# Sinkhorn weights loaded one expert ahead, block sums and input preparation a step sooner, and another order of the tail

## The chip, the cores and the metric

The kernel runs on one core of a Trainium2 chip. A core has a matrix engine (TensorE, PE in the profile; PEld are its weight loads), a vector engine (VectorE, DVE), an activation engine (ScalarE, ACT), a general engine (GpSimd, POOL) and a small engine whose queue here issues most of the DMA transfers (SyncE, SP). Each engine works through its own instructions in order and waits on semaphores where it needs another's result. The metric is the device time of one execution in microseconds; the lower the better.

## The reference

2304 tokens of 512 channels pass through three stages. The attention has random features and is no part of what follows.

```python
def _moe_ref(x, w_gate, w1, w2):           # MoE1: 8 experts, all of them for every token
    P = np.exp(logits - max)               # logits = x @ w_gate
    for _ in range(8):                     # Sinkhorn: rows and columns in turn
        P /= P.sum(1, keepdims=True) + 1e-09
        P /= P.sum(0, keepdims=True) + 1e-09
        P *= N / E
    for e in range(E):
        out += P[:, e:e+1] * (np.maximum(x @ w1[e], 0.0) @ w2[e])
def _moe2_ref(x, w_skip, w_gate, w1, w2):  # MoE2: one expert per token
    do = x @ w_skip > 0                    # the other tokens pass unchanged
    e_idx = argmax(x[do] @ w_gate)         # gate = softmax value of the chosen expert
    out[do] = x + gate * (np.maximum(x @ w1[e_idx], 0.0) @ w2[e_idx])
```

w1[e] is 512x1024 and w2[e] 1024x512, in float32.

## The kernel before

**Tiling.** Float32 operands are split into a high and a low part, and each product is made of three matmuls (high by high, high by low, low by high). The 2304 tokens are 18 tiles of 128, in 6 groups of 3 (384 columns) and 3 passes of 6 tiles. MoE1 is a loop over 96 steps n = (pass p, expert e, i), 4 steps per expert, 32 per pass. Pass 0 (to step 31) also builds block combinations of the weights and keeps them in DRAM (`w1c`, `w2c`). Passes 1 and 2 (steps 32 to 63 and 64 to 95) run `fast` with these: seven block products in place of eight, both for x@w1 (`product`, L291) and for h@w2 (`prod2`, L996). In a fast step TensorE runs the seven `product` of step n and, as `sec`, the seven `prod2` of step n-1. The mark of a step in the trace is ScalarE's copy at L1085, after the first product.

**Weighing.** Since the second product is linear, the Sinkhorn weight P[token, e] is put on the hidden block: `weigh` applies relu on ScalarE (L1048) and multiplies on GpSimd by `pw` (L1049). `pw` is one expert's weights for the pass's 768 tokens, spread over all 128 partitions. `load_pw` (L967) reads it from DRAM by one DMA of 384 KB, in rows of 512 bytes. Then come combinations on GpSimd (`comb`, L1053), the split into high and low part (`hi_a` on ScalarE, L1058; `lo_a` on VectorE, L1061), and the block products. Their sums are added into the block buffers `ebuf` by VectorE (L1017).

**SyncE's queue.** All weights come through SyncE's queue in program order: `fetch_w1(n+1)` at a step's start (four DMAs, L160), `fetch_w2(n+1)` behind the step's code (L174, L176). Each DMA waits there until its buffer is free, and holds those behind it. In the kernel before `load_pw` has one buffer and stands behind `fetch_w2` in the last step of an expert (i == 3), for the step that follows.

**Between passes.** `prep_x` (L248) makes the seven input blocks of the next pass during the last expert's steps; its first piece is three subtractions on GpSimd (L258 to L260). `fin` (L1022) combines the block sums of a pass into its output: five pieces, each run by a `next(fz, None)` in the step after the first of the new pass (step 65 for pass 1), and after the loop for pass 2. `route(g)` chooses the experts of MoE2 for a group; its pieces run whenever `pump()` is called, three times per fast step.

**Tail.** After the last step come its `prod2`, `fin(2)`, the last routing pieces, and MoE2 in slots of up to 128 tokens of one expert. Slots 0 and 1 have a known expert and run beside the last routing. `load_slot` loads w1 and w2 as halves `r1[0]`, `r1[1]`, `r2[0]`, `r2[1]`, for slot 0 from GpSimd's queue; `split` makes the parts (cast on ScalarE L1283, low part L1284); `xsplit` transposes and splits a slot's tokens (L1304 to L1306); `products` (L1294) are 12 or 6 matmuls. The count of tokens per expert (L1396) is turned on VectorE (L1399 to L1436) into registers, from which slots 2 and on take their expert.

Of the kernel before, what the change touches and what calls it, by code (L numbers as in the profile page):

```python
# [21 lines left out]
def attn_moe_moe_kernel(  # L22
# [645 lines left out]
    ps_y = yst.enter_context(tc.tile_pool(name="ps_y", bufs=1, space=PSUM))  # L668
# [231 lines left out]
    def second(n, t):  # L900
        if not 0 <= n < ns_:
            return
        p, e, i = steps[n]
        if i == 0:
            ys[t] = ps_y.tile([P, DM], F32, tag=f"y{t}", name=f"y{t}")
# [12 lines left out]
        if i < KI - 1:  # L918
            return
        T = p * 2 * GT + t  # L920
        sc = Pm[:, T, e : e + 1]
        if e == 0:
            acc[t] = ebuf[0][:, t, :]
            if p == 0:
                nc.scalar.copy(acc[t], ys[t])
            else:
                nc.vector.tensor_scalar(acc[t], ys[t], sc, None, OP.mult)
        else:
            if p == 0 and e == 1:
# [56 lines left out]
    def prod2(n, j):  # L986
        if not yb:
            yb.extend(ps_y.tile([P, DM], F32, tag=f"y{t}", name=f"y{t}") for t in range(2 * GT))
# [30 lines left out]
    def fin(p):  # L1019
        eb = ebuf[p % 2]  # L1020
        e1, e6, e7, e5 = eb[:, :GT, :D2], eb[:, :GT, D2:], eb[:, GT:, :D2], eb[:, GT:, D2:]
        add = lambda o, x: nc.vector.tensor_tensor(o, x, o, OP.add)  # L1022
# [8 lines left out]
        yield  # L1031
        add(e7, e6)
        yield
        add(e6, e5)
        add(e5, e7)
# [31 lines left out]
    def fast(n, x_next, fz, pump):  # L1067
# [31 lines left out]
        pump()  # L1099
# [53 lines left out]
    for n, (p, e, i) in enumerate(steps):  # L1153
# [7 lines left out]
        if e == E - 1 and p + 1 < NP:  # L1161
# [37 lines left out]
        if p:  # L1199
            fz = fin(p - 1) if p > 1 and e == 0 and i == 1 else iter(())  # L1200
            fast(n, x_next, fz, pump)
            fetch_w2(n + 1)
            if i == KI - 1:
                load_pw(*steps[n + 1][:2]) if n + 1 < ns_ else None
            continue

        def after(k):
# [7 lines left out]
            if k == 5 and 1 < n < N0 - 1:  # L1215
                split_sum_w2(n)
# [15 lines left out]
    for a in (1, 6, 5):  # L1232
        split_a2(ns_ - 1, a)
# [3 lines left out]
    wst.close()  # L1237


    z_p = ctx.enter_context(tc.tile_pool(name="z", bufs=1))  # L1240
    w_p = ctx.enter_context(tc.tile_pool(name="wz", bufs=9))
    NS = FF // 2
    KH = KF // 2

# [3 lines left out]
    xn += pair([P, DM], F32, "xn3", 3 - NE)  # L1248
    xhs = pair([P, KD, P], F32R, "xhs")
    xls = pair([P, KD, P], F32R, "xls")  # L1250
# [4 lines left out]
    r2 = pair([P, KH, DM], F32, "r2")  # L1255
    r1 = pair([P, KD, NS], F32, "r1")

    def load_slot(e, cond, eng=nc.sync):
        for i in range(4):
# [39 lines left out]
    def xsplit(s):  # L1299
        if s == NSLOT:  # L1300
            return
        px = m_bank()
        for c in range(KD):
            nc.tensor.transpose(px[:, c * P : (c + 1) * P], xn[s % 3][:, c * P : (c + 1) * P], ident)  # L1304
        nc.scalar.copy(xhs[s % 2], px)
        nc.vector.tensor_tensor(  # L1306
            xls[s % 2], px.rearrange("p (c t) -> p c t", c=KD), xhs[s % 2].bitcast(F32), OP.subtract
        )

    wa, wb = {}, {}  # L1310

    def split_a(s, r, c):
        if not 0 < s < NE:
            wa[c, r] = split(r1[r][:, c, :], "w1", nc.gpsimd if (r, c) in ((0, 3), (1, 0), (1, 3)) else nc.vector)
# [6 lines left out]
    def slot(s):  # L1321
        x = (xhs[s % 2], xls[s % 2])
        py = pys[s % 2]
# [17 lines left out]
        p1 = ps_1.tile([P, 512], F32, tag="p1", name="p1")  # L1341
# [10 lines left out]
        p1 = ps_1.tile([P, 512], F32, tag="p1", name="p1")  # L1352
# [6 lines left out]
        yield  # L1359
        products(py, hts[0], lambda c: wb[c], h0, True, False)  # L1360
# [10 lines left out]
    load_slot(reg_at(reg0, 0, [ET.Pool], E - 1), None, nc.gpsimd)  # L1371
# [4 lines left out]
    for s in range(NE):  # L1376
        xsplit(s)
    for _ in fin(NP - 1):
# [18 lines left out]
    next(early[0])  # L1397
# [40 lines left out]
    for _ in early[0]:  # L1438
        pass
# [49 lines left out]
```

## Time and profile before

| what | value |
|---|---|
| median of 3 runs | 1956.0 us (1951.95 to 1956.86) |
| the profiled execution | 1957.7 us |
| its span, first to last instruction | 1956.1 us |
| TensorE busy | 1826.4 us (93%) |
| VectorE busy | 1390.6 us (71%) |
| GpSimd busy | 899.4 us (46%) |
| ScalarE busy | 864.0 us (44%) |
| granted TensorE clock, mean | 0.966 |

Times in the views are microseconds from the span's start. A row of the timeline gives start, duration, engine, line, operation, written tile <- read tiles, shape, count of merged instructions, and in brackets the idle time before it with what released it. A row of the waits gives engine, tile and line that waited, what it waited for, total, times and longest. Granted clock 1.00 is TensorE at full speed.

### The profile page before, as it was taken

What the parts mean: (1) busy time and instruction counts of PE and PEld (TensorE: products, weight loads), DVE (VectorE), ACT (ScalarE), POOL (GpSimd) and SP (SyncE); (2) the same over time, 40 slices, a digit from 0 to 9 for tenths busy, and PEclk for the clock granted to TensorE, in tenths of its full rate; (3) what the DMA queues carried; (4) which work ended last, traced back from release to release, by engine and by line L of the source; (5) the groups of instructions that cost most, each with busy time, mean ns of one, the idle gap of its engine ahead of it and who ended that gap; (6) DMA issues with size and microseconds to landing.
All of it is one profiled execution on the core that took longest, in us unless ns stands there. A gap on an engine that the chain in (4) does not pass through costs nothing. (4 is left out here: it accounts for less than half of the span.)

```text
span 1956.1 us, 31251 instructions
## 1 busy us (share of the span) xinstructions
PE 1826.4 (93%) x11395; PEld 1706.4 (87%) x11395; DVE 1390.6 (71%) x2437; ACT 864.0 (44%) x1856; POOL 899.4 (46%) x876
## 2 busy tenths in 40 slices
PE   8999988999999989999999999888999999999598
PEld 8888777888888878999999999878999999999576
DVE  7768466776677776677667777866777777777577
ACT  5758443444444453343334333432343433334356
POOL 5232134444455453444444444634454444445257
PEclk9989999999999999999999999989999999999799
DMA  7230657888888989667666767556576676665441
GB/s 194 72 91 28 215 207 270 294 294 291 306 307 305 330 314 334 196 244 255 218 223 229 251 224 261 205 185 245 190 246 232 234 259 235 230 238 192 151 165 67
DMA packets 221940, 441.41 MB, mean 226 GB/s; under 512 B 25272, under 2 KB 119576, under 8 KB 221776
## 3 DMA queue, kind: packets, MB, share of 16 engines
q1 hardware_dynamic: 218656, 431.70, 63.9%
q0 software_dynamic: 3120, 7.61, 1.1%
q8 instruction: 92, 1.51, 0.3%
q14 instruction: 72, 0.59, 0.1%
HBM read 320.71 MB, written 132.07 MB: 231 GB/s over the span
## 5 line engine op out<-in xcount | busy, mean ns | idle before, releaser
L291 PE MATMUL m<-xh,w1h 128*128 128x384 f32 x1330 | 456.9, 343 | 16.4 <-DVE c L345 3.0
L291 PE MATMUL m<-xl,w1h 128*128 128x384 f32 x1330 | 453.3, 341 | 0.0
L291 PE MATMUL m<-xh,w1l 128*128 128x384 f32 x1330 | 452.8, 340 | 0.0
L1049 POOL TENSOR_TENSOR c<-c,pw 128x384 f32<-128x384 f32 x192 | 195.2, 1017 | 519.4 <-ACT c L1048 427.0
L291 PEld LDWEIGHTS m<-xh,w1h 128*128 128x128 f32 x1330 | 256.1, 193 | 31.6 <-DVE rc L697 6.2
L996 PE MATMUL y<-w2h,hh 128*128 128x256 f32 x768 | 226.1, 294 | 46.0 <-DVE eb L1017 41.3
L1017 DVE TENSOR_TENSOR eb<-y,eb 128x256 f32<-128x256 f32 x496 | 254.1, 546 | 15.2 <-PE y L996 14.8
L291 PEld LDWEIGHTS m<-xl,w1h 128*128 128x128 f32 x1330 | 256.0, 192 | 8.2
L1061 DVE TENSOR_TENSOR hl<-s,hh 128x384 fp32r<-128x384 f32 x256 | 230.6, 901 | 37.4 <-ACT hh L1058 35.0
L291 PEld LDWEIGHTS m<-xh,w1l 128*128 128x128 f32 x1330 | 254.6, 191 | 0.6 <-DMA w1l<-w1c 0.6
L1061 DVE TENSOR_TENSOR hl<-c,hh 128x384 fp32r<-128x384 f32 x192 | 143.0, 745 | 136.9 <-ACT hh L1058 136.7
L996 PE MATMUL y<-wb,hh 128*128 128x256 f32 x1152 | 220.5, 290 | 4.3 <-DVE eb L1022 2.0
L996 PE MATMUL y<-w2l,hh 128*128 128x256 f32 x768 | 218.8, 285 | 0.0
L996 PE MATMUL y<-w2h,hl 128*128 128x256 f32 x768 | 218.5, 285 | 0.0
L996 PEld LDWEIGHTS y<-w2h,hh 128*128 128x128 f32 x768 | 146.9, 191 | 60.7 <-DVE eb L1017 53.3
L996 PEld LDWEIGHTS y<-wb,hh 128*128 128x128 f32 x1152 | 191.1, 197 | 6.5 <-DVE eb L1022 2.4
L1058 ACT CAST hh<-c 128x384 fp32r<-128x384 f32 x192 | 98.7, 514 | 221.4 <-POOL c L1049 221.4
L1048 ACT ACTIVATE c<-c 128x384 f32<-128x384 f32 x192 | 100.9, 526 | 176.9 <-DVE c L1131 80.3
L1058 ACT CAST hh<-s 128x384 fp32r<-128x384 f32 x256 | 129.9, 509 | 111.2 <-POOL s L1053 111.2
L996 PE MATMUL y<-wb,hl 128*128 128x256 f32 x576 | 165.8, 288 | 0.0
L216 POOL TENSOR_TENSOR wsum<-raw 128x256 f32<-128x256 f32 x32 | 29.4, 919 | 284.7 <-DVE w1l L234 250.1
L1053 POOL TENSOR_TENSOR s<-c,c 128x384 f32<-128x384 f32 x128 | 149.0, 1164 | 14.8 <-DVE c L1123 10.4
(300 smaller groups left out, 3878.5 us busy)
## 6 DMA issues: line engine op xcount, KB each, us to landing
wb<-w2c SPq DMA_DIRECT2D x128, 384.0 KB
w1h<-w1c SPq DMA_DIRECT2D x64, 640.0 KB
w1l<-w1c SPq DMA_DIRECT2D x64, 640.0 KB
w2h<-w2c SPq DMA_DIRECT2D x64, 512.0 KB
w2l<-w2c SPq DMA_DIRECT2D x64, 512.0 KB
w2c<-eb SPq DMA_DIRECT2D x58, 512.0 KB
w1c<-w1h SPq DMA_DIRECT2D x32, 896.0 KB
w1c<-w1l SPq DMA_DIRECT2D x32, 896.0 KB
```

What stands on the lines that cost most here:

```text
L216: nc.gpsimd.tensor_tensor(sm[:, 0], a21, a22, OP.add)
L291: nc.tensor.matmul(ps[:, :GW], x[:, a, c, :], y[:, c, :], start=first and m == 0, stop=m == 3 * KC - 1, skip_group_check=True,)
L996: nc.tensor.matmul(place(k, t), x[:, ts], y,  start=m == 0 and (own or (k, t) == (2, 2) or e == i == 0 and (k, t) in FIRST), stop=m == 2 a ...
L1017: nc.vector.tensor_tensor(dst, src, dst, OP.add)
L1048: nc.scalar.activation(out=t, in_=t, func=AF.Relu)
L1049: nc.gpsimd.tensor_tensor(t, t, pw[steps[n][:2]][:, g], OP.mult)
L1053: nc.gpsimd.tensor_tensor(t, ct[n, x], ct[n, y], op)
L1058: nc.scalar.copy(ha[n, a][0], ct[n, a])
L1061: nc.vector.tensor_tensor(ha[n, a][1], ct[n, a], ha[n, a][0].bitcast(F32), OP.subtract)
```

## The change

There are seven edits.

1. `load_pw` takes its tile from a pool with two buffers, and is called after the first step of expert e for expert e+1, ahead of `fetch_w2`.
2. For one of the two pass changes the first piece of `prep_x` runs in step 62 in place of 63.
3. `fin` of pass 1 makes two of its additions on GpSimd, and two pieces are merged and one is divided.
4. `pump()` is called twice per fast step.
5. In pass 0 the split of summed w2 is done one product earlier (k == 4).
6. In step 88 GpSimd issues the load of slot 0's first half of w1 into the block buffer that is free by then.
7. In the tail slot 0's tokens are split before the last `prod2`; the accumulators of `prod2` are in two pools, so that one is given back early and slot products have banks (`ps_p`) before `fin`; slot 0's first products and slot 1's tokens come before `fin`, all of slot 0 before the count; the memory of `r1[1]`, `xhs` and `xls` is placed first.

```diff
-    ps_y = yst.enter_context(tc.tile_pool(name="ps_y", bufs=1, space=PSUM))
+    tst = ExitStack()
+    ps_y = [yst.enter_context(tc.tile_pool(name="ps_y", bufs=1, space=PSUM))] * (2 * GT)
+    ps_y[2] = ps_y[3] = tst.enter_context(tc.tile_pool(name="ps_t", bufs=1, space=PSUM, side="right"))
...
     def load_pw(p, e):
         if p < NP:
-            t = c_p.tile([P, 2, GW], F32, tag="pw", name="pw", bufs=1)
+            t = w_p.tile([P, 2, GW], F32, tag="wsum", name="pw")
...
-    def fin(p):
+    def fin(p, eng):
...
         add(e6, e1)
         yield
         add_y(e1, 0)
-        yield
         add(e7, e6)
         yield
-        add(e6, e5)
-        add(e5, e7)
+        add(e6, e5, eng)
+        add(e5, e7, eng)
+        yield
         add_y(e7, 2)
         yield
...
         sec(0)
-        pump()
         product(py, 4, 4, n, False)
...
                 nxt[2] = prep_x(nxt[0], nxt[1], xq)
+                if p:
+                    next(nxt[2])
             if i == KI - 1:
                 xp = nxt[2]
-                next(xp)
+                if not p:
+                    next(xp)
...
-            fz = fin(p - 1) if p > 1 and e == 0 and i == 1 else iter(())
+            fz = fin(p - 1, nc.gpsimd) if p > 1 and e == 0 and i == 1 else iter(())
             fast(n, x_next, fz, pump)
+            if i == 0 and n + KI < ns_:
+                load_pw(*steps[n + KI][:2])
             fetch_w2(n + 1)
-            if i == KI - 1:
-                load_pw(*steps[n + 1][:2]) if n + 1 < ns_ else None
+            if n == ns_ - 2 * KI:
+                w1b_0 = w1b[bass.ds(reg_at(reg0, 0, [ET.Pool], E - 1), 1)].rearrange("o (c p) f -> p (o c) f", p=P)
+                nc.gpsimd.dma_start(ebuf[1][:, :KD], w1b_0[:, :, : FF // 2])
             continue
...
-    for a in (1, 6, 5):
-        split_a2(ns_ - 1, a)
+    x0 = xr_p.tile([P, 2, KD, P], F32R, tag="xr", name="x0")
+    xhs, xls = [x0[:, 0]], [x0[:, 1]]
+    r1 = [ebuf[1][:, :KD, :]]
...
+    split_a2(ns_ - 1, 1)
+    xsplit(0)
+    split_a2(ns_ - 1, 6)
+    split_a2(ns_ - 1, 5)
     for j in range(7):
         prod2(ns_ - 1, j)
     mst.close()
     wst.close()
+    tst.close()
...
+            pool = ((0, 3), (1, 0), (1, 3)) if s else ((0, 0), (0, 1), (1, 0), (1, 3))
+            wa[c, r] = split(r1[r][:, c, :], "w1", nc.gpsimd if (r, c) in pool else nc.vector)
...
-    load_slot(reg_at(reg0, 0, [ET.Pool], E - 1), None, nc.gpsimd)
+    load_slot(reg_at(reg0, 0, [ET.Pool], E - 1), None, nc.gpsimd, 1)
...
-    for s in range(NE):
-        xsplit(s)
-    for _ in fin(NP - 1):
+    xsplit(1)
+    early = [slot(s) for s in range(NE)]
+    next(early[0])
+    for _ in fin(NP - 1, nc.vector):
         pass
...
-    early = [slot(s) for s in range(NE)]
     last = [route(NG - 2), route(NG - 1)]
+    for _ in range(2):
+        next(early[0])
...
-    for _ in range(3):
-        next(early[0])
+    for _ in early[0]:
+        pass
...
     nc.tensor.matmul(pm[:1, :E], ones[:, 0:1], cnt[0], start=True, stop=True)
-    next(early[0])
...
-    for _ in early[0]:
-        pass
```

**SyncE at the first step of an expert (step 48).** In the kernel before its queue has these rows; w1h, w1l are the weights of the next step's first product, w2h, w2l and wb those of the second, pw the Sinkhorn weights.

```order
L176 DMA wb_10764<-w2c 128x768
L176 DMA wb_10765<-w2c 128x768
L967 DMA pw<-ptd 128x6x128
L160 DMA w1h<-w1c 128x512
L160 DMA w1l<-w1c 128x512
L160 DMA w1h<-w1c 128x1280
L160 DMA w1l<-w1c 128x1280
L174 DMA w2h<-w2c 128x1024
L174 DMA w2l<-w2c 128x1024
```

After the change the same place reads so.

```order
L176 DMA wb_10769<-w2c 128x768
L176 DMA wb_10770<-w2c 128x768
L160 DMA w1h<-w1c 128x512
L160 DMA w1l<-w1c 128x512
L160 DMA w1h<-w1c 128x1280
L160 DMA w1l<-w1c 128x1280
L969 DMA pw<-ptd 128x6x128
L174 DMA w2h<-w2c 128x1024
```

The load of pw has gone from ahead of the four w1 loads to behind them, and it is now the one for the expert after this.

**GpSimd at the change from step 62 to 63.** The kernel before has the first piece of `prep_x` (L258 to L260) behind the last combinations of step 62.

```order
L1049 TENSOR_TENSOR c_13411<-c_13411,pw 128x384
L1053 TENSOR_TENSOR s<-c_13411,s 128x384
L1053 TENSOR_TENSOR s<-c_13375,c_13472 128x384
L258 TENSOR_TENSOR eb_3036<-xr 128x768
L259 TENSOR_TENSOR eb_3036<-xr,eb_3036 128x768
L260 TENSOR_TENSOR eb_3036<-xr 128x768
L1049 TENSOR_TENSOR c_13562<-c_13562,pw 128x384
```

After the change it stands behind the combinations of step 61, ahead of the first weighing of step 62.

```order
L1051 TENSOR_TENSOR c_13232<-c_13232,pw 128x384
L1055 TENSOR_TENSOR s<-c_13232,s 128x384
L1055 TENSOR_TENSOR s<-c_13196,c_13293 128x384
L258 TENSOR_TENSOR eb_3039<-xr 128x768
L259 TENSOR_TENSOR eb_3039<-xr,eb_3039 128x768
L260 TENSOR_TENSOR eb_3039<-xr 128x768
L1051 TENSOR_TENSOR c_13383<-c_13383,pw 128x384
```

The weighings are L1049 before and L1051 after, the combinations L1053 and L1055; the three subtractions come seven rows sooner among them.

**TensorE in the tail, from the last block product on.** In the kernel before the tokens of both slots are transposed there (L1304), and products of slot 0 (p, L1294) alternate with the transposes of the routing (L721, which read the block buffer that `fin` finishes).

```order
L996 MATMUL y_7889<-wb_19693,hl 128x256
L1304 MATMUL m<-ident,xn 128x128 x8
L1294 MATMUL p_20042<-w1h,xhs_19965 128x512
L1294 MATMUL p_20042<-w1h,xls_19967 128x512
L1294 MATMUL p_20042<-w1l,xhs_19965 128x512
L721 MATMUL m<-ident,eb_3036 128x128 x4
L1294 MATMUL p_20042<-w1h,xhs_19965 128x512
```

After the change, from the last block product, the rows are these.

```order
L998 MATMUL y_7894<-wb_19700,hl 128x256
L1251 MATMUL m<-ident,xn 128x128 x4
L1323 MATMUL p_20032<-w1h,x_19876 128x512 x2
L1323 MATMUL p_20032<-w1l,x_19876 128x512
L1323 MATMUL p_20032<-w1h,x_19876 128x512 x2
L1323 MATMUL p_20032<-w1l,x_19876 128x512
L1323 MATMUL p_20032<-w1h,x_19876 128x512 x2
```

The slot's products (L1323) now follow without a routing transpose between them, so they depend on `fin` no more; the routing's transposes come only behind the first three products of the second product (py).

## Rows read from the trace of the kernel before

**Rows 1.** The waits of TensorE: total us, times, longest us.
```profile
PE y L996 <- DVE eb L1017: 41.8, 17, 4.1
PE p L1294 <- DVE eb L1022: 16.1, 1, 16.1
...
PE y L996 <- DVE eb L1022: 6.7, 3, 2.7
...
PE m L765 <- DVE c L1094: 6.6, 1, 6.6
```

**Rows 2.** The waits of all engines, the row of pw.
```profile
POOL c L1049 <- DMA pw<-ptd: 92.4, 15, 9.6
```

**Rows 3.** Windows of steps 41 to 43, summed (us, then busy by engine).
```profile
sum 45.09, PE 45.09 PEld 44.40 DVE 36.20 ACT 18.87 POOL 23.22; mean PE 15.03 PEld 14.80 DVE 12.07 ACT 6.29 POOL 7.74
```

**Rows 4.** Windows: step 48, and 13 first steps summed; last columns PEclk, DMA, GB/s.
```profile
1003.53:1024.15 20.62, 16.50 (x105) 16.09 (x104) 11.48 (x22) 6.27 (x14) 8.36 (x8) 0.92 0.58 196
...
sum 247.24, PE 211.74 PEld 205.31 DVE 148.64 ACT 81.04 POOL 107.07; mean PE 16.29 PEld 15.79 DVE 11.43 ACT 6.23 POOL 8.24
```

**Rows 5.** The timeline of step 42 (first two rows) and step 48.
```profile
910.62 1.02 POOL L1049 TENSOR_TENSOR c<-c,pw 128x384 f32<-128x384 f32 x1 [1.52 <-ACT c L1048]
...
915.18 0.32 SPq L174 DMA_DIRECT2D w2h<-w2c  x1
...
1003.10 0.37 SPq L967 DMA_DIRECT2D pw<-ptd  x1
...
1013.07 0.99 POOL L1049 TENSOR_TENSOR c<-c,pw 128x384 f32<-128x384 f32 x1 [7.30 <-DMA pw<-ptd]
...
1014.63 0.56 DVE L1061 TENSOR_TENSOR hl<-c,hh 128x384 fp32r<-128x384 f32 x1 [6.59 <-ACT hh L1058]
...
1015.58 0.48 PE L996 MATMUL y<-w2h,hh 128*128 128x256 f32 x1 [4.12 <-DVE eb L1017]
```

**Rows 6.** Windows: steps 32 and 33, then parts of steps 42 and 48.
```profile
733.02:771.35 38.33, 34.12 (x208) 31.41 (x209) 25.10 (x46) 13.38 (x30) 15.15 (x15) 0.98 0.99 340
...
909.36:912.36 3.00, 3.00 (x23) 3.00 (x22) 2.83 (x6) 1.69 (x4) 1.02 (x1) 1.00 0.95 322
...
1006.00:1009.00 3.00, 3.00 (x23) 3.00 (x23) 2.04 (x5) 1.20 (x3) 0.00 (x0) 1.00 0.50 107
```

**Rows 7.** The window of step 63, and its timeline on GpSimd and VectorE.
```profile
1249.27:1273.51 24.24, 18.47 (x107) 17.43 (x106) 19.86 (x26) 11.31 (x22) 17.99 (x12) 0.86 0.45 151
...
1251.47 2.59 POOL L258 TENSOR_TENSOR eb<-xr 128x768 f32<-128x768 f32 x1
...
1252.26 2.23 DVE L1061 TENSOR_TENSOR hl<-s,hh 128x384 fp32r<-128x384 f32 x1
...
1256.16 1.84 POOL L260 TENSOR_TENSOR eb<-xr 128x768 f32<-128x768 f32 x1
```

**Rows 8.** The timeline of VectorE in step 65.
```profile
1300.10 1.94 DVE L1022 TENSOR_TENSOR eb<-eb 128x768 f32<-128x768 f32 x2
```

**Rows 9.** The timeline of the tail.
```profile
1824.52 3.13 POOL L1265 DMA_DIRECT2D r<-in_moe_w_dram  x4 [9.13 <-PE y L996]
...
1830.26 2.18 ACT L1283 CAST w1h<-r 128x512 fp32r<-128x512 f32 x4 [14.33 <-DMA r<-in_moe_w_dram]
...
1841.14 0.77 PE L1294 MATMUL p<-w1h,xhs 128*128 128x512 f32 x1 [16.06 <-DVE eb L1022]
...
1848.99 0.50 PE L1294 MATMUL p<-w1h,xhs 128*128 128x512 f32 x1 [1.19 <-ACT w1h L1283]
...
1850.35 0.50 PE L1294 MATMUL p<-w1l,xhs 128*128 128x512 f32 x1 [0.62 <-POOL w1l L1284]
...
1859.79 0.19 PE L1396 MATMUL m<-cn,ones 128*1 128x8 f32 x2 [2.08 <-DVE cn L755]
...
1866.16 0.15 DVE L1399 COPY nn<-m 1x8 f32<-1x8 f32 x1
...
1881.71 0.39 PE L1294 MATMUL p<-w1h,xhs 128*128 128x512 f32 x1
```

More of the change, by code (lines that the diff above doesn't have):

```diff
@@ L904, in second @@
         if i == 0:
-            ys[t] = ps_y.tile([P, DM], F32, tag=f"y{t}", name=f"y{t}")
+            ys[t] = ps_y[t].tile([P, DM], F32, tag=f"y{t}", name=f"y{t}")
         ts = slice(t % GT * P, (t % GT + 1) * P)
@@ L987, in prod2 @@
         if not yb:
-            yb.extend(ps_y.tile([P, DM], F32, tag=f"y{t}", name=f"y{t}") for t in range(2 * GT))
+            yb.extend(ps_y[t].tile([P, DM], F32, tag=f"y{t}", name=f"y{t}") for t in range(2 * GT))
         p, e, i = steps[n]
@@ L1017, in prod2 @@
                 nc.vector.tensor_tensor(dst, src, dst, OP.add)
-    def fin(p):
+    def fin(p, eng):
         eb = ebuf[p % 2]
         e1, e6, e7, e5 = eb[:, :GT, :D2], eb[:, :GT, D2:], eb[:, GT:, :D2], eb[:, GT:, D2:]
-        add = lambda o, x: nc.vector.tensor_tensor(o, x, o, OP.add)
+        add = lambda o, x, eng=nc.vector: eng.tensor_tensor(o, x, o, OP.add)
         def add_y(o, k):
@@ L1214, in after @@
                 sum_w2(n, raw2[n])
-            if k == 5 and 1 < n < N0 - 1:
+            if k == 4 and 1 < n < N0 - 1:
                 split_sum_w2(n)
@@ L1231, in attn_moe_moe_kernel, with xbuf, xsplit @@
             fetch_w2(n + 1)
-    for a in (1, 6, 5):
-        split_a2(ns_ - 1, a)
+    x0 = xr_p.tile([P, 2, KD, P], F32R, tag="xr", name="x0")
+    xhs, xls = [x0[:, 0]], [x0[:, 1]]
+    r1 = [ebuf[1][:, :KD, :]]
+    def xbuf(s):
+        return 1 + s % 2 if s else 0
+    def xsplit(s):
+        if s == NSLOT:
+            return
+        px = m_bank()
+        for c in range(KD):
+            nc.tensor.transpose(px[:, c * P : (c + 1) * P], xn[s % 3][:, c * P : (c + 1) * P], ident)
+        j = xbuf(s)
+        nc.scalar.copy(xhs[j], px)
+        nc.vector.tensor_tensor(xls[j], px.rearrange("p (c t) -> p c t", c=KD), xhs[j].bitcast(F32), OP.subtract)
+    split_a2(ns_ - 1, 1)
+    xsplit(0)
+    split_a2(ns_ - 1, 6)
+    split_a2(ns_ - 1, 5)
     for j in range(7):
@@ L1237, in attn_moe_moe_kernel @@
     wst.close()
-    z_p = ctx.enter_context(tc.tile_pool(name="z", bufs=1))
-    w_p = ctx.enter_context(tc.tile_pool(name="wz", bufs=9))
+    tst.close()
     NS = FF // 2
     KH = KF // 2
+    z_p = ctx.enter_context(tc.tile_pool(name="z", bufs=1))
     def pair(shape, dt, nm, n=2):
         return [z_p.tile(shape, dt, name=f"{nm}_{i}") for i in range(n)]
-    xn += pair([P, DM], F32, "xn3", 3 - NE)
-    xhs = pair([P, KD, P], F32R, "xhs")
-    xls = pair([P, KD, P], F32R, "xls")
+    r1 += pair([P, KD, NS], F32, "r1", 1)
+    xhs += pair([P, KD, P], F32R, "xhs")
+    xls += pair([P, KD, P], F32R, "xls")
+    w_p = ctx.enter_context(tc.tile_pool(name="wz", bufs=9))
+    z_p = ctx.enter_context(tc.tile_pool(name="zb", bufs=1))
+    r2 = pair([P, KH, DM], F32, "r2")
     os_ = pair([P, DM], F32, "os")
@@ L1254, in attn_moe_moe_kernel, with load_slot @@
     hls = pair([P, KH, P], F32R, "hl")
[L1255 to L1259, printed above, removed]
+    xn += pair([P, DM], F32, "xn3", 3 - NE)
+    ps_p = ctx.enter_context(tc.tile_pool(name="ps_p", bufs=2, space=PSUM, side="right"))
+    def load_slot(e, cond, eng=nc.sync, first=0):
+        for i in range(first, 4):
             r = i % 2
@@ L1297, in products @@
                 next(fill.popleft())
[L1299 to L1308, printed above, removed]
     wa, wb = {}, {}
@@ L1313, in split_a @@
         if not 0 < s < NE:
-            wa[c, r] = split(r1[r][:, c, :], "w1", nc.gpsimd if (r, c) in ((0, 3), (1, 0), (1, 3)) else nc.vector)
+            pool = ((0, 3), (1, 0), (1, 3)) if s else ((0, 0), (0, 1), (1, 0), (1, 3))
+            wa[c, r] = split(r1[r][:, c, :], "w1", nc.gpsimd if (r, c) in pool else nc.vector)
     def split_b(s, *cs):
@@ L1321, in slot @@
     def slot(s):
-        x = (xhs[s % 2], xls[s % 2])
-        py = pys[s % 2]
+        x = (xhs[xbuf(s)], xls[xbuf(s)])
         hts = list(zip(hhs, hls))
@@ L1340, in slot @@
             split_a(s, 0, c)
-        p1 = ps_1.tile([P, 512], F32, tag="p1", name="p1")
+        p1 = ps_p.tile([P, 512], F32, tag="p1", name="p1")
         products(p1, x, lambda c: wa[c, 0], range(KD), True, True)
@@ L1351, in slot @@
         split_b(s, *h0)
-        p1 = ps_1.tile([P, 512], F32, tag="p1", name="p1")
+        p1 = ps_p.tile([P, 512], F32, tag="p1", name="p1")
         products(p1, x, lambda c: wa[c, 1], range(KD // 2), True, False)
@@ L1359, in slot @@
         yield
+        py = pys[s % 2]
         products(py, hts[0], lambda c: wb[c], h0, True, False)
```

## The prediction

> **What bounds the kernel now.** The page comes first: TensorE is busy for most of the span, so time is lost only where it stands, and where it works at a lower clock after it stood. The view of TensorE's waits names those places [rows 1]. The longest entry is 41.8 us in 17 waits of the block products (L996) for VectorE's additions into the block buffers (L1017); then come one wait of 16.1 us at the first product of MoE2 and entries of about 7 us. A name in that view is only the last releaser. Reading back one step, GpSimd waited 92.4 us in 15 waits at its weighing (L1049) for the DMA of `pw` [rows 2].
>
> The windows show what that costs. An ordinary fast step, from one L1085 to the next, lasts 45.09/3 = 15.03 us with TensorE busy all the time [rows 3]. The 13 first steps of an expert (36 to 60 and 72 to 92, every fourth) last 247.24 us together, of which TensorE is busy 211.74; 13 ordinary ones would last 195.4. The excess is 51.9 us: 35.5 us of standing, 16.4 us of longer matmuls at a lower granted clock (0.92 in step 48) [rows 4].
>
> The timeline of step 48 shows the way from the DMA to TensorE [rows 5]. SyncE issues `pw` at 1003.10, 0.43 us before the step begins, because in its queue the load stands behind `wb`, whose buffers come free late in the step before. The weighing starts at 1013.07, 9.5 us into the step; in the ordinary step from 906.86 it starts at 910.62, 3.8 us in, and waits for ScalarE only. So it is 5.8 us late and the step 5.6 us long: nearly all of the delay is paid, and TensorE resumes at 1015.58 after standing for 4.12.
>
> **The load of pw.** The new place in SyncE's queue is behind the four w1 loads of the first step of expert e, for expert e+1. Nothing else is added: one DMA of 384 KB (393 kB) per expert as before, one buffer more. At that place the queue was free: the w2 loads behind it go out only 8.3 us into the ordinary step, at 915.18 [rows 5], and the buffer that pw takes was last read an expert earlier. If the transfer takes the 10 us from issue to use of [rows 5], it is there about 14 us into the step, and it is needed three steps later. The wait goes whole. What is late next is nothing on that path: TensorE is full in ordinary steps [rows 3], and the first step of an expert does the same work. Term: -52. If half of the low-clock excess stayed (8 us) it would be -44; the upper end is -55. The two other waits among the 15 lie at the passes' starts, where other work is late too: between 0 and two mean excesses (8 us), I take -2, since routing and block sums still hold those steps.
>
> The load for the second expert of pass 1 now runs in steps 32 and 33, where the DMA engines are busy 0.99 at 340 GB/s and TensorE is busy 34.12 of 38.33 us [rows 6]. 393 kB cost 1.2 us at 340 GB/s, 3.7 us at the 107 GB/s at which pw's packets ran in step 48 [rows 6], 10 us if all of its issue-to-use time showed, and 0 if weights arrive with slack. I take +3, near the row with the same packets.
>
> The Trainium skill, "DMA: Bandwidth & Descriptors", § Specifications, gives 512 bytes as the smallest transfer at line rate, and pw's rows are of 512 bytes. The 107 GB/s beside the 322 GB/s of a w1 stretch does not bear that out here; by the rule the term would be +1.2, and the rival on w1 below would have no ground.
>
> **The inputs of the next pass a step sooner.** Three subtractions on GpSimd (2.59 for the first, 1.84 for the last, 6.5 us for the three) move from the start of step 63 to the start of step 62 for one of the two pass changes [rows 7]. In 63 they hold back its first weighing until 1258.0, 8.7 us into a step that lasts 24.24. In 62 they will hold back that step's first weighing as long, some 5 us past 3.8. By [rows 5] that costs 62 about 4.5 us, and 63, which had the same delay, gets about as much back. Term 0; if the cost in 62 stays and 63 gains nothing because its ten other operations fill it, +4.5; if 62 hides it, -4.5.
>
> **Block sums a step sooner.** The two additions that take VectorE 1.94 us in step 65 go to GpSimd, and one yield is moved so that the buffers in PSUM are emptied earlier [rows 8]. TensorE waits for these sums 6.7 us in 3 waits [rows 1]. The part of it that can go is at most that, and the least is nothing, since the later sums now wait for GpSimd, where an operation of that size takes about 2 us, and behind them in GpSimd's queue stands the next weighing; a late weighing costs nearly its delay [rows 5], so +2 bounds it above. I take -1.
>
> In step 63 a VectorE subtraction with two SBUF inputs took 2.23 us from 1252.26 and ended just after GpSimd's L258, against 0.56 for the same subtraction in step 48, where GpSimd stands idle [rows 5, 7]. The Trainium skill, "SBUF — State Buffer", § Who interferes with whom, says that such a pair excludes one another: the later of the two is blocked until the first is through. By that rule the two additions on GpSimd hold VectorE for as long as they free it, and this term is 0 or +2.
>
> **Small edits.** One call of the routing generator less per step lets the same routing work come in longer bursts: 0, at most the 6.6 us that a routing product waits now either way [rows 1], I use 2. In pass 0 one split of w2 goes one product earlier in steps in which TensorE is full: 0, by 2 either way. The 1 MB load in step 88 sits on GpSimd's queue, where each issue costs 0.8 us [rows 9]: +0.5, at most +1. The first slot's transposes now stand ahead of the last block products: +0.5.
>
> **The tail.** All times from 1825.08, when TensorE falls idle (16.06 before 1841.14) [rows 9]. Now GpSimd starts issuing the four loads at 1824.52, when the last block products free the memory; the first lands for ScalarE at 1830.26 (+5.2). VectorE makes the low parts and runs `fin` behind them, and TensorE goes on at 1841.14 (+16.1), because the accumulators must be freed before the products' banks exist. The count comes at 1859.79 (+34.7), but VectorE turns to it only at 1866.16 (+41.1), as it holds splits of slot 0 that wait for ScalarE. From this reading come the registers, slot 2's loads and its start at 1881.71 (+56.6). What follows is a regular row of slots, so the tail's gain is what moves this point.
>
> After the change the first half of w1 is there from step 88, and products have banks of their own. ScalarE's four casts (2.18) start at once: -5.2. Against it `fin` now also stands behind two more splits of w1's second half, for which two casts and a split are late, +1.1. So `fin` ends at about +12: -4.1. TensorE works beside it, and what it waited for ScalarE's and GpSimd's second half (1.19 and 0.62 us from 1847.8 to 1850.4) falls into that time: -1.8. The count is put behind all products of slot 0, so VectorE has no split ahead of it: of the 6.4 us between count and its reading some 0.3 remain: -6.1. Slot 1's 48 products must then cover the 15.6 us from reading to slot 2, as in the rows of before. Sum -12. If the load of the second half lands 8 us later than `fin` needs it, the gain of the splits is lost, since VectorE's queue is in order: -5. If TensorE also keeps its clock through the gap, -16.
>
> Sum: -52 - 2 + 3 + 0 - 1 + 0.5 + 0.5 - 12 = -63. The profiled execution took 1957.7 us (its span is 1.6 shorter), the median of the runs 1956.0. 1957.7 - 63 = 1894.7, less 1.7: **1893 us**. The ends together (-44, +6, -5 against -55, -5, -16) give 1880 to 1915 for this case.
>
> **Rivals.**
> (a) Half of the stalls remain, because pw's small packets, now in flight with the w1 of the next step, make that w1 late, or because something else holds a first step. For it: the first steps' stretch runs at 107 GB/s with pw in it, an ordinary one at 322 [rows 6]. Against: 1792 KB of w1 take 5.7 us at 322 GB/s, so it has the rest of the step, about 9 us. 26 of 52 stay: 1920, up to 1945. Chance 0.12.
> (b) More is gained: 62 and 63 together lose the 4.5, the waits at the passes' starts go (8), the tail gives 16. 1865 to 1880. Chance 0.06.
> (c) The load is not ahead in fact, since the new buffer comes free late and SyncE waits with the w2 loads behind it. Only the tail remains: 1945; if the tail's load lands late as well, 1951, which is no change. Chance 0.04, most of it on the second.
> (d) Slower: w1 is held by pw beyond the step's end. It decides from the point where w1 lands over 4.6 us too late in each of 14 steps (64 us), that is at +19.6 in place of +5.7. At 6 us each it costs 84 against a gain of 64: 1977. The row of [rows 5] has all of pw through in 10 us with w1 in the same queue, so 15 us are unlikely. Chance 0.04.
>
> The forecast has 0.74. A measurement of this kernel can tell 0.3%, about 5.9 us, from no change. Faster: forecast, (a), (b) and a part of (c), 0.93; same 0.03; slower 0.04. The range reaches a little into (a) and (b): 1878 to 1922.
>
> **What will show it.** GpSimd's wait for `pw` is gone from the waits, TensorE's entry at L1017 falls below 10 us, first steps of experts last 15.0 to 15.2 us at full granted clock. Steps 62 and 63 together last about 39 us, step 62 alone 19 to 20. TensorE's gap in the tail is under 8 us and slot 2 starts about 44 us after it falls idle. The prediction is wrong if TensorE waits for `w1h` in the step after an expert's first, if GpSimd still waits for `pw`, or if VectorE stands in the tail for the second half's load.

## The result and the profile after

The changed kernel takes 1907.0 us, median of 4 runs (1901.74 to 1907.9); the kernel before took 1953.97 us beside it (1951.85 to 1956.86). The ratio is 0.9753, with a 95% interval of 0.9729 to 0.9777: 47 us or 2.5% faster. Forecast were 63 us (1893), in a range that holds the time (1878 to 1922). The profiled execution is the 1901.74 us one, with a span of 1900.1 and a mean granted clock of 0.974 (0.966 before).

The waits of TensorE in the changed kernel (total us, times, longest us) begin with other rows than before [rows 1].

```profile
PE m L291 <- DMA w1h<-w1c: 9.2, 1, 9.2
PE y L998 <- DVE eb L1019: 8.2, 6, 3.0
...
PE y L998 <- DVE eb L1024: 6.1, 3, 2.3
PE pt L1350 <- DVE eb L1024: 5.2, 1, 5.2
```

The 41.8 us at the block additions are 8.2 now. Of GpSimd's 15 waits for `pw` one is left, in step 32, at the start of pass 1, whose load stands where it stood:

```profile
POOL c L1051 <- DMA pw<-ptd: 4.8, 1, 4.8
```

Two waits have come up: 9.2 us for weights in one place (3.0 before), and 5.2 us for `fin` in the tail, in place of the 16.1. So slot 0 does depend on `fin`: its first 18 products run ahead of it, but the transposes of its hidden block (L1350) need PSUM banks that `fin` gives back. The windows of step 48 and of the 13 first steps of experts (the columns as in [rows 4]) show the stall gone:

```profile
996.25:1011.27 15.02, 15.02 (x107) 14.82 (x106) 12.03 (x21) 6.29 (x15) 7.88 (x8) 1.00 0.85 274
...
sum 196.87, PE 196.87 PEld 194.50 DVE 156.17 ACT 81.69 POOL 99.91; mean PE 15.14 PEld 14.96 DVE 12.01 ACT 6.28 POOL 7.69
```

TensorE is busy in all of it, at full granted clock but for step 36 (0.95). In the timeline pw for step 48 leaves SyncE's queue in step 44, behind the w1 loads, and the weighing of step 48 starts 3.75 us into the step, waiting for ScalarE, as in an ordinary step [rows 5].

```profile
937.39 0.37 SPq L969 DMA_DIRECT2D pw<-ptd  x1
...
1000.00 1.01 POOL L1051 TENSOR_TENSOR c<-c,pw 128x384 f32<-128x384 f32 x1 [1.52 <-ACT c L1050]
```

The two profiled spans, cut at the steps' marks, differ so (us):

| stretch | before | after | difference | forecast |
|---|---|---|---|---|
| to the mark of step 32 | 733.0 | 726.9 | -6.1 | 0 |
| steps 32 to 35 | 76.3 | 86.7 | +10.4 | +3 |
| steps 36 to 61 and 70 to 94 | 819.5 | 768.9 | -50.6 | -52 |
| steps 62 and 63 | 39.3 | 39.3 | 0.0 | 0 |
| steps 64 to 69 | 130.4 | 126.0 | -4.4 | -3 |
| from the mark of step 95 | 157.5 | 152.3 | -5.3 | -11 |

The sum is -56, 9 us more than between the medians: the profiled execution of after was the fastest of its four, and that of before, with 1957.7, lay above its four. How much two executions differ is seen in the attention, which no edit touches: over the 14 profiled kernels it ended, by the first addition of pass 0, between 187.0 and 194.4 us. Of the -6.1 of the first row, 2.5 lie there (194.2 before, 191.8 after).

Three of the six rows are off: the four steps at the start of pass 1, the tail, and pass 0.

In steps 33 and 34 (before, first, then after; columns as in [rows 4]) the time goes to a wait and to work at a lower clock.

```profile
748.77:771.35 22.58, 19.70 (x138) 18.97 (x137) 15.03 (x31) 7.54 (x17) 9.25 (x10) 0.97 0.99 346
771.35:788.50 17.15, 17.15 (x119) 17.08 (x119) 10.69 (x26) 6.66 (x15) 8.88 (x10) 0.94 0.76 254
```

```profile
741.49:768.49 27.00, 17.12 (x115) 16.59 (x114) 14.25 (x22) 7.39 (x17) 9.65 (x9) 0.86 0.87 319
768.49:791.05 22.56, 22.28 (x134) 22.18 (x135) 11.33 (x28) 6.31 (x15) 5.88 (x7) 0.79 0.55 200
```

Step 33 has 23 matmuls fewer than before and yet lasts 4.4 us longer; step 34 has 15 more, at a granted clock of 0.79, and lasts 5.4 us longer. What moved are the 24 small routing products (128x9, L728 before and L730 after). Their share of TensorE's time in step 33 before, and in steps 33 and 34 after:

```profile
748.77:771.35 22.58, 2.74 (x24) 2.82 (x24) 0.97 0.99 346
...
741.49:768.49 27.00, 0.24 (x2) 0.56 (x3) 0.86 0.87 319
768.49:791.05 22.56, 4.88 (x23) 4.78 (x23) 0.79 0.55 200
```

Most of the 5.4 us is their 4.88. Some eight other matmuls of the routing go from there on to step 35, which lasts 22.6 us in place of 20.9.

The timeline of the tail in the changed kernel, to compare with [rows 9]. The last block product ends at 1773.7.

```profile
1773.72 2.18 ACT L1312 CAST w1h<-eb 128x512 fp32r<-128x512 f32 x4 [8.48 <-PE y L998]
1775.41 6.07 DVE L1313 TENSOR_TENSOR w1l<-eb,w1h 128x512 fp32r<-128x512 f32 x1 [1.00 <-ACT w1h L1312]
1775.96 2.53 POOL L1313 TENSOR_TENSOR w1l<-eb,w1h 128x512 fp32r<-128x512 f32 x2
1778.43 2.49 POOL L1313 TENSOR_TENSOR w1l<-r,w1h 128x512 fp32r<-128x512 f32 x2
...
1783.81 0.95 DVE L1024 TENSOR_TENSOR eb<-eb 128x768 f32<-128x768 f32 x1
...
1789.04 1.61 DVE L1024 TENSOR_TENSOR eb<-y,eb 128x512 f32<-128x512 f32 x3
...
1790.80 1.09 PE L1350 MATMUL pt<-ident,hb 128*128 128x128 f32 x4 [5.17 <-DVE eb L1024]
...
1809.54 0.20 PE L1417 MATMUL m<-cn,ones 128*1 128x8 f32 x2 [2.08 <-DVE cn L757]
...
1809.77 0.15 DVE L1419 COPY nn<-m 1x8 f32<-1x8 f32 x1 [0.38 <-PE m L1417]
...
1825.70 0.39 PE L1323 MATMUL p<-w1h,xhs 128*128 128x512 f32 x1
```

ScalarE's casts start at once, as forecast, and the count is read 0.2 us after it is made, in place of 6.4. But one subtraction of VectorE takes 6.07 us, from 1775.41 to 1781.48, just as long as GpSimd is at its four; so `fin` starts at 1783.81, 10.1 us behind the last block product, and in the kernel before that was 9.9. The additions of `fin` in the kernel before, first and last, with its last block product ending at 1824.2:

```profile
1834.16 0.95 DVE L1022 TENSOR_TENSOR eb<-eb 128x768 f32<-128x768 f32 x1
...
1839.38 1.61 DVE L1022 TENSOR_TENSOR eb<-y,eb 128x512 f32<-128x512 f32 x3
```

Counted from the last block product, `fin` ends at 17.0 (16.8 before), the count is made at 35.9 (35.6 before), and slot 2 starts at 52.0 (57.5 before). So the 5.5 us come from the count's being read sooner, and none from `fin`.

Times below are medians beside the kernel before on the same chip, and a ratio is compared with the changed kernel's 0.9753; what the intervals can't tell is read from windows. One run of experiment 5, of 2482.1 us, is left out of its median and its ratio.

### The profile page after: what moved, and what is told of

It is laid out like the page before. It is cut to its first block, busy times and chain, and to the rows that moved or that the text cites. A ratio compares the mean times of both kernels' runs of the same rounds, so it can differ in the third digit from the quotient of the medians.

```text
span 1900.1 us, 31306 instructions
## 1 busy us (share of the span) xinstructions
PE 1814.2 (95%) x11395; PEld 1695.0 (89%) x11395; DVE 1388.0 (73%) x2434; ACT 867.7 (46%) x1856; POOL 887.3 (47%) x879
## 5 line engine op out<-in xcount | busy, mean ns | idle before, releaser
L1051 POOL TENSOR_TENSOR c<-c,pw 128x384 f32<-128x384 f32 x192 | 195.1, 1016 | 455.2 <-ACT c L1050 450.4
L1063 DVE TENSOR_TENSOR hl<-s,hh 128x384 fp32r<-128x384 f32 x256 | 243.1, 950 | 35.8 <-ACT hh L1060 33.0
L998 PE MATMUL y<-wb,hh 128*128 128x256 f32 x1152 | 213.6, 284 | 5.0 <-DVE e L1019 2.7
L998 PEld LDWEIGHTS y<-wb,hh 128*128 128x128 f32 x1152 | 185.4, 191 | 5.8 <-DVE e L1019 3.2
L1055 POOL TENSOR_TENSOR s<-c,c 128x384 f32<-128x384 f32 x128 | 151.2, 1182 | 8.4 <-DVE c L1124 3.7
```

The costliest lines, as they stand in the source:

```text
L998: nc.tensor.matmul(place(k, t), x[:, ts], y,  start=m == 0 and (own or (k, t) == (2, 2) or e == i == 0 and (k, t) in FIRST), stop=m == 2 a ...
L1051: nc.gpsimd.tensor_tensor(t, t, pw[steps[n][:2]][:, g], OP.mult)
L1055: nc.gpsimd.tensor_tensor(t, ct[n, x], ct[n, y], op)
L1063: nc.vector.tensor_tensor(ha[n, a][1], ct[n, a], ha[n, a][0].bitcast(F32), OP.subtract)
```

## The experiments

**1. The load in its old place, with two buffers.**

```diff
-            if i == 0 and n + KI < ns_:
-                load_pw(*steps[n + KI][:2])
             fetch_w2(n + 1)
+            if i == KI - 1:
+                load_pw(*steps[n + 1][:2]) if n + 1 < ns_ else None
```

> The changed kernel with the load of pw back behind fetch_w2 in the last step of an expert; all else as changed. Theory A, the load's place is the source of the gain: the wait of GpSimd for pw returns with about 90 us, the 13 first steps take about 50 us more, and the time rises to 1945-1957 us. Rival, the gain comes from other edits (buffers, block sums, tail): the time stays below 1915 us. For steps 32 to 35, theory P (pw's transfer in step 33 holds back w1 of step 34): the wait of 9.2 us falls to 3 us or less and the four steps last 76-80 us. Rival Q (the routing moved by the dropped pump call lets TensorE arrive before w1): the wait stays and the four steps last 85-88 us.

1925.8 us, ratio 0.9865 (0.9828 to 0.9902): neither. The windows of the 13 first steps, summed, and GpSimd's wait for pw in this kernel:

```profile
sum 221.92, PE 206.23 PEld 199.80 DVE 148.55 ACT 81.12 POOL 99.35; mean PE 15.86 PEld 15.37 DVE 11.43 ACT 6.24 POOL 7.64
```

```profile
POOL c L1051 <- DMA pw<-ptd: 69.0, 15, 6.5
```

The excess over 195.4 is 26.5 us, half of the 51.9, with the load where it was. Two pump calls alone bring the first steps from 247.2 to 243.2 (the kernel of experiment 4), 3.0 of it in step 36. For the other 21 us the buffer is what differs there. The windows of the 13 first steps with two pump calls alone, summed:

```profile
sum 243.17, PE 211.44 PEld 205.89 DVE 150.49 ACT 81.40 POOL 105.37; mean PE 16.26 PEld 15.84 DVE 11.58 ACT 6.26 POOL 8.11
```

SyncE's timeline at the change to step 48 in the kernel before, and GpSimd's beside it:

```profile
997.64 4.67 SPq L176 DMA_DIRECT2D wb<-w2c  x2
1003.10 0.37 SPq L967 DMA_DIRECT2D pw<-ptd  x1
...
1002.06 1.02 POOL L1049 TENSOR_TENSOR c<-c,pw 128x384 f32<-128x384 f32 x1 [1.16 <-ACT c L1048]
```

The queue is through with `wb` at 1002.31, but pw goes out at 1003.10, when the last weighing of step 47, which reads the single buffer, ends (1003.08). With two buffers it goes out at 997.05, 1.1 us ahead of the mark in place of 0.43, right behind `wb`. The first use comes 7.6 us into step 48, in place of 9.5: 0.7 of these 2.0 us are the earlier issue, and why the way from issue to use is 1.3 shorter as well is not shown. The second buffer alone, in the kernel before, was not run. On the four steps: 82.7, wait for w1h 5.1; between P and Q.

**2. The first early load in step 34.** In the changed kernel `load_pw(1, 1)` is called in step 34 (`n == N0 + 2`) and not in step 32.

> The changed kernel, but the first of the early loads (pass 1, second expert) is issued in step 34 in place of step 32. Theory P: the wait of TensorE for w1h at the start of step 34 falls from 9.2 us to 3 us or less, steps 32 to 35 last 77-81 us in place of 86.7, and the time is 6 to 9 us lower, 1898-1901 us. Rival Q: wait and time unchanged, 1905-1908 us.

1898.9 us, ratio 0.9734 (0.9707 to 0.9761). Steps 32 to 35 last 83.0 in place of 86.7, step 33 is back at 23.0, and the wait for w1h is 5.1 in place of 9.2. The kernels with the changed kernel's code in these steps (experiments 5, 6 and 9) took 85.9, 89.0 and 88.1 there. So pw's transfer costs 3 to 6 us (3 were forecast), and something else keeps the other 7; P holds for a part, since the wait stays above its 3 us.

**3. The third pump call in the changed kernel.**

```diff
         sec(0)
+        pump()
         product(py, 4, 4, n, False)
```

> The changed kernel with the third call of the routing generator restored in every fast step. Rival Q: in steps 32 to 35 the routing spreads as in the kernel before, the wait for w1h falls to 3 us or less, the four steps last 76-80 us, and the time is 6 to 9 us lower. Theory P: the wait for w1h stays at 7 us or more, and the time stays within 3 us of 1907. In steps 67 to 69, where the changed kernel was 1.5 us shorter, up to 2 us may come back in either case.

1899.4 us, ratio 0.9736 (0.9707 to 0.9765). The windows of steps 33 and 34:

```profile
743.25:770.09 26.84, 21.32 (x138) 20.79 (x137) 15.82 (x32) 7.60 (x18) 9.64 (x10) 0.86 0.86 319
770.09:787.58 17.49, 17.49 (x119) 17.41 (x119) 10.79 (x26) 6.68 (x15) 8.90 (x10) 0.92 0.72 241
```

Step 33 lasts as long as without the call (27.0), with the 23 routing matmuls in it, and step 34 is 5.1 us shorter without them. The four steps last 79.7. Steps 67 to 69 last 71.0 (67.8 in the changed kernel, 67.4 to 69.8 in the other kernels with the change and two calls there), steps 64 to 66 gain 1.6, which is within scatter. The wait for w1h is 4.8, so Q holds for the routing and not for the wait.

**4. The kernel before with two pump calls.** The same call taken out of the kernel before, nothing else.

> The kernel before with one of the three pump calls taken out, nothing else. Theory R (the dropped call moves routing out of step 33, which waits for weights anyway, into step 34): TensorE has about 115 matmul groups in step 33 in place of 138, step 34 lasts 21-23 us in place of 17.2, steps 32 to 35 together 79-84 in place of 76.3, and steps 67 to 69 are 1 to 3 us shorter; the time is 1 to 5 us above the kernel before. Rival (the routing's place costs nothing, and the 7 us seen with the changed kernel come from the load in step 32 alone): steps 32 to 35 at 75-78 us.

1958.1 us, ratio 1.0031 (1.0016 to 1.0046): 0.3% slower, the interval just clear of 1. Steps 32 to 35 last 85.1, a little above the range; the windows of 33 and 34:

```profile
748.16:771.11 22.95, 16.93 (x113) 16.45 (x112) 13.87 (x21) 7.26 (x17) 9.51 (x9) 0.90 0.99 354
771.11:793.45 22.34, 22.06 (x134) 21.97 (x135) 11.33 (x28) 6.32 (x14) 5.88 (x7) 0.80 0.55 203
```

Theory R holds by its windows: step 33 is as long with 113 matmuls as with 138, because it ends when the weights of step 34 have come through DMA engines that are busy 0.99; step 34 pays 5.2 us, and step 35 another 2.8. Steps 67 to 69 were 0.7 longer, not shorter.

**5. All low parts of slot 0's w1 on VectorE.**

```diff
-            pool = ((0, 3), (1, 0), (1, 3)) if s else ((0, 0), (0, 1), (1, 0), (1, 3))
+            pool = ((0, 3), (1, 0), (1, 3)) if s else ()
```

> The changed kernel, but all eight low parts of slot 0's w1 are made on VectorE and none on GpSimd. Theory T (VectorE's first two low parts took 6.67 us since GpSimd's four ran beside them): eight low parts take about 0.65 us each, 5 us together, fin starts about 2.5 us sooner, TensorE's wait of 5.2 us for fin falls to about 2.5, and the time is 2 to 4 us lower, 1903-1905 us. Rival (ScalarE's casts or the loads set that pace): VectorE waits for w1h instead, fin starts no sooner, 1906-1909 us.

1900.2 us, ratio 0.9737 (0.9705 to 0.9769); the intervals overlap, so the reading is the tail's. In its timeline the four low parts of the first half take 2.50 us and `fin` starts 6.1 us behind the last block product, at 1774.74:

```profile
1769.32 2.50 DVE L1313 TENSOR_TENSOR w1l<-eb,w1h 128x512 fp32r<-128x512 f32 x4
1771.74 0.68 DVE L1254 TENSOR_TENSOR xls<-m,xhs 128x512 fp32r<-128x512 f32 x1
...
1774.74 0.95 DVE L1024 TENSOR_TENSOR eb<-eb 128x768 f32<-128x768 f32 x1
...
1779.98 1.61 DVE L1024 TENSOR_TENSOR eb<-y,eb 128x512 f32<-128x512 f32 x3
...
1800.57 0.19 PE L1417 MATMUL m<-cn,ones 128*1 128x8 f32 x2 [2.08 <-DVE cn L757]
...
1816.26 0.39 PE L1323 MATMUL p<-w1h,xhs 128*128 128x512 f32 x1
```

Theory T holds, and by more than expected: `fin` comes 4.0 us sooner though VectorE has twice the low parts to make, and from the mark of step 95 the rest takes 148.1 us (152.3). The four kernels with the low parts on VectorE (experiments 5, 6, 11 and 12) take 148.1 to 151.0 there, the six with the changed kernel's split 152.2 to 154.6. TensorE's wait for `fin` grows to 7.5, since it is through its first products sooner.

**6. fin ahead of the second half.** As 5, with a yield that puts `fin` ahead of the split of w1's second half and of slot 1's tokens.

> The changed kernel with slot 0's low parts on VectorE, and with the additions of fin put ahead of the split of w1's second half and of slot 1's tokens. Theory T continued (fin's start is set by what stands ahead of it on VectorE): fin starts 3 us sooner than with the low parts on VectorE alone, slot 2 starts about 44.5 us after the last block product (52.0 in the changed kernel, 47.6 with the low parts on VectorE), and the time is 6 to 8 us below the changed kernel's. Rival (the products of the second half then stand on the path): slot 2 at 47 us or later.

1898.2 us, ratio 0.9730 (0.9709 to 0.9751). `fin` starts 3.1 us behind the last block product, 3.0 sooner than in 5, but slot 2 starts at 46.5, only 1.2 sooner: TensorE waits 4.8 us for a low part of the second half in place of `fin`. The rest from the mark of step 95 takes 150.3, no less than in 5. So moving `fin` further up shows no gain, and 46.5 is nearer the rival's 47 than the theory's 44.5.

**7. Long rows in the kernel before.** The weights are stored by expert, then tile.

```diff
-    ptd = tc.dram_tile([NT - 2 * GT, E, P], F32, name="ptd")
+    ptd = tc.dram_tile([E, NT - 2 * GT, P], F32, name="ptd")
...
-                t.rearrange("p g (t n) -> p (g t) n", n=P),
-                ptd[T0 : T0 + 2 * GT, e, :].partition_broadcast(P),
+                t.rearrange("p g n -> p (g n)"),
+                ptd[e, T0 : T0 + 2 * GT, :].rearrange("t n -> (t n)").partition_broadcast(P),
```

> The kernel before, with one thing changed: the weights lie in DRAM by expert, then tile, so that pw is read in 128 rows of 3072 bytes in place of 768 of 512 (the weights are put in that order by one small copy before they are written). Place and buffer of the load are those of before. Theory S (the small rows set the transfer's time): the transfer takes 2 to 3 us in place of 7 to 8, GpSimd's wait for pw falls from 92 us to under 25, the 13 first steps lose most of their 52 us of excess, and the time falls to 1905-1920 us. Rival (the load's place behind other transfers sets it): the wait stays above 60 us and the time is within 15 us of the kernel before.

1905.4 us, ratio 0.9778 (0.9749 to 0.9808): nearly as much as the whole change brings, with the load in its old place and one buffer. The windows of the 13 first steps, summed, and the timeline of pw's way into step 48:

```profile
sum 200.35, PE 200.03 PEld 195.74 DVE 146.44 ACT 81.53 POOL 100.11; mean PE 15.39 PEld 15.06 DVE 11.26 ACT 6.27 POOL 7.70
```

```profile
986.96 0.32 SPq L970 DMA_DIRECT2D pw<-ptd  x1
...
992.73 1.01 POOL L1052 TENSOR_TENSOR c<-c,pw 128x384 f32<-128x384 f32 x1 [3.54 <-DMA pw<-ptd]
```

5.8 us from issue to use in place of 10.0 (over the 13 first steps 5.5 in the mean, 4.9 to 6.1, in place of 8.6, 6.9 to 10.0), and 5 us of excess in place of 52. Theory S holds for the time, though not for the 2 to 3 us that it gave the transfer. GpSimd's wait is still 47.3 us in 14 waits, against the 25 expected: most of it costs TensorE nothing, which loses 5 us in these steps.

**8. Long rows in the changed kernel.**

> The changed kernel with the same long rows. Theory P with S: the wait for w1h at the start of step 34 falls from 9.2 us to about 5, as with the load in step 34, steps 32 to 35 last 83-84 us, and the time is 3 to 4 us lower; the first steps of experts stay at 15.0. Rival (bytes, not rows, cost there): wait and time unchanged.

1900.4 us, ratio 0.9735 (0.9709 to 0.9760). Steps 32 to 35 last 84.5 (86.7), the wait for w1h is 6.4. The direction is that of P with S, the size 2.3 us; neither the interval nor the windows can tell it from nothing, since the kernel of experiment 5, with short rows, took 85.9 with a wait of 6.6.

**9. The block sums of step 65 back on VectorE.** `fin(p - 1, nc.vector)` in the changed kernel.

> The changed kernel with the two moved additions of the block sums back on VectorE in step 65; the moved pieces stay. If the moved pieces alone shortened steps 64 to 66 (61.1 before, 58.2 after): the three steps last 57-59 us and the time is unchanged. If GpSimd's taking the additions did it: 60-61 us and 2 to 3 us more in all. The six runs of kernels with the same code there lie between 56.6 and 58.9 us, with one at 59.6, so a smaller difference than 2 us says nothing.

1901.4 us, ratio 0.9753 (0.9728 to 0.9778), the same as the changed kernel's. Steps 64 to 66 last 59.0 (58.2): the engine of the two additions makes no difference that shows. In the changed kernel GpSimd's two took 3.94 us, and VectorE's next subtractions 1.46 and 2.20, in place of some 0.55 each.

**10. One edit of pass 0 alone.** The kernel before with the split of summed w2 one product earlier.

```diff
-            if k == 5 and 1 < n < N0 - 1:
+            if k == 4 and 1 < n < N0 - 1:
```

> The kernel before with the split of summed w2 in pass 0 one product earlier (k == 4), nothing else. If that edit is what shortens steps 2 to 8 of pass 0 (116.3 us in the kernel before, 109.5 to 112.2 in the kernels with the change): the six steps last 110-112 us, TensorE's wait in the Sinkhorn products (m, L695) falls from 7.2 to about 4 us, and the time is 3 to 6 us lower, ratio 0.997 to 0.9985. If another edit does it (the pools of the accumulators): the steps stay at 116 and the time is unchanged.

1945.4 us, ratio 0.9954 (0.9931 to 0.9978): 0.5% faster, the interval clear of 1. The windows of the six steps (from an addition at L318 to the sixth after it) in the kernel before, and in this one:

```profile
236.11:352.41 116.30, 105.49 (x493) 90.27 (x492) 80.52 (x161) 46.94 (x91) 44.13 (x51) 0.96 0.67 243
```

```profile
231.47:341.11 109.64, 101.09 (x491) 87.91 (x490) 78.76 (x161) 47.13 (x91) 40.42 (x49) 0.98 0.70 253
```

6.7 us less, of which 0.6 is given back by the mark of step 32. TensorE's wait in the Sinkhorn products falls from 7.2 to 4.1.

**11. The repairs together.** The changed kernel with 2, 5, 8, and the third pump call in pass 1 alone.

> The changed kernel with long rows for pw, its first early load in step 34, slot 0's low parts on VectorE, and the third pump call in pass 1 alone. If the three repairs add up (about -4 to -5, -4, and -7 in steps 32 to 35 with no loss in 67 to 69): steps 32 to 35 last 76 us or less, steps 67 to 69 about 68, the tail from the mark of step 95 takes 148, and the time is 12 to 16 us below the changed kernel's. If pump and load mend the same wait: 32 to 35 at 79-80 and 9 to 11 us below.

1882.2 us, ratio 0.9654 (0.9630 to 0.9679): 1.0% below the changed kernel's ratio, and the intervals do not overlap. Steps 32 to 35 last 72.8, 67 to 69 67.4, and the tail 148.8. The repairs add up, to somewhat more than expected.

**12. The same with the load in its old place**, and two buffers.

> The combined kernel (long rows, low parts on VectorE, third pump call in pass 1) with the load of pw behind fetch_w2 in the last step of an expert, as in the kernel before, but with the second buffer. Theory S (with long rows the place is worth little): the 13 first steps last 15.0 to 15.6 us, up to 4 us more in all, steps 32 to 35 stay at 72-74 us, and the time is 0 to 4 us above the combined kernel's. Rival (the place matters by itself): the first steps last 16 us or more, 13 us or more in all.

1888.3 us, ratio 0.9679 (0.9655 to 0.9703). The 13 first steps sum to 197.5 (196.7 in 11), steps 32 to 35 to 74.3. With long rows the place is worth about 1 us there; the rest of the 6 us between the medians lies in scatter and in a tail that took 2.2 us longer.

## Why the forecast held, and where it did not

**The load of pw.** Right in place and size: -52 forecast, -50.6 measured. The reason was half of it. The step "in its queue the load stands behind `wb`, whose buffers come free late" names only one of two things that held the load: the last weighing still read its one buffer (experiment 1), and with a second buffer some 21 of the 52 us go, the place unchanged. And what made the load long was its layout in 768 rows of 512 bytes (experiment 7): with 128 rows of 3072 bytes, place and buffer as before, 47 of the 52 us go. The forecast did not ask why the load was slow; its place was enough to mend it, but it was not the only thing that was. The Trainium skill, "DMA: Bandwidth & Descriptors", § Specifications, gives 512 bytes as the smallest transfer at line rate. By that the row size would have changed little; in step 48 it took the load from 10.0 to 5.8 us.

**Steps 32 and 33.** The term of +3 for the load was near: taking it away gives 3.7 back, 3 to 6 against the other kernels with this code (experiment 2). The other +7 come from the step by which fewer calls let "the same routing work come in longer bursts: 0". It looked at the length of the routing's waits and not at where its matmuls stand. Step 33 ends when weights arrive; what TensorE does ahead of that cost nothing here, and the dropped call moves 23 matmuls from there into step 34, where they cost 5 us (experiments 3 and 4), and others into step 35, where they cost 2 to 3. What came back in steps 64 to 69 (126.0 to 127.6 and 129.2 to 130.4 with two calls to three) is within scatter: the five kernels with the changed kernel's code there lie between 125.9 and 128.4.

**Inputs and block sums a step sooner.** Step 62 took 19.40 us, step 63 19.92 (15.05 and 24.23 before): +4.4 and -4.3, the term of 0 with both its halves. In steps 64 to 69 -3 were forecast and -4.4 measured; over the five kernels with this code and the three with that of before the means are 126.7 and 129.7. Experiment 9 finds no part of GpSimd's in it. The rule in the Trainium skill's "SBUF — State Buffer", § Who interferes with whom, would have it so, and the trace agrees: VectorE's subtractions beside GpSimd's two additions took 1.46 and 2.20 us.

**The tail.** -12 forecast, and +0.5 twice beside it; -5.3 measured. The step that failed is "`fin` ends at about +12: -4.1", and with it the -1.8 for waits that would fall into that time. Casts and loads were on time, but the four low parts given to GpSimd stopped VectorE for 6.07 us, and `fin` ended 17.0 us behind the last block product, as before (16.8). The prediction had the rows and the rule for this and used them for step 65 alone; the same rule stands against the tail's split. The part for the count was right: -6.1 forecast, 6.1 measured (6.37 us from count to reading before, 0.23 after). With VectorE alone `fin` ends at 13.0 (1781.59 in experiment 5), the -4.1 but for 0.3, and slot 2 starts 47.6 us behind the last block product; the forecast's 44 us, counted from where TensorE falls idle, are 45.5 on this scale. What is left is the -1.8. From `fin`'s end to the count there are 18.8 us before, 18.9 after and 19.0 in experiment 5: of slot 0's first products 18 have gone ahead of `fin`, but its 24 second products, which stood behind the count, now stand ahead of it. The prediction priced neither move, only the waits.

**Pass 0.** The step "in steps in which TensorE is full: 0" was wrong in its ground: in six early steps, where Sinkhorn products run between the blocks, TensorE is busy 105.5 of 116.3 us and waits for VectorE, and a split issued sooner shortens them (experiment 10). Why the order on VectorE helps there was not followed further.

**The total.** The two errors, 7 us too few in steps 32 to 35 and 6 too few in the tail, go the same way. Pass 0, forecast at nothing, gave 4 to 6 of them back, which was luck.

**The rivals.** (a), w1 late by pw, happened after one of the 15 early loads, the one into steps whose DMA engines were full, and in part (5.1 of the 9.2 us stay when pw is gone, experiment 2); there the prediction's own sign of being wrong came, TensorE waiting for `w1h` in the step after an expert's first. (b), more gained, did not occur, nor did (c) and (d): the w1 loads ahead of pw were not held up.

## What to carry to other kernels

Before a load is moved out of the way, ask why it is slow: here a layout with rows of 3 KB did nearly as much as a load one expert ahead. Work that ran in a step which ended on a transfer was free, so an edit that only moves such work is priced by the step that receives it. The same holds for work that is put ahead of the point on which the rest depends. And work given to GpSimd beside VectorE is priced by what VectorE does in the same microseconds, in every place, not in one.

## What was not expected of the hardware

A VectorE subtraction with both inputs in SBUF started 0.55 us ahead of the first of four such GpSimd subtractions and ended 0.56 us behind the last: 6.07 us in place of 0.68, and 6.06 to 6.07 in all six kernels with this split. It got no turn between GpSimd's instructions, though it started first; GpSimd's took 1.27 to 1.30 us each, no more than in the tail of before (1.28 to 1.43).

384 KB spread over 128 partitions took 10.0 us from issue to use in 768 rows of 512 bytes, and 5.8 us in 128 rows of 3072 bytes, from the same place in the same queue (step 48; over the 13 first steps 6.9 to 10.0 and 4.9 to 6.1). Each row is read once for every partition, and four loads of w1 go out right behind it, so this is no rate of a transfer by itself.
